# The hand-written order of tasks past the head is made anew (S5 scan and channel MLP, one Trainium2 core)

## The chip, the cores and the metric

The kernel runs on one core of one Trainium2 chip. The metric is device time in microseconds (us) of one execution. Five engines with a queue each carry the work: PE (TensorE, matmuls), ACT (ScalarE), DVE (VectorE), POOL (GpSimd) and SP (SyncE, which here only issues DMAs). An engine works through its own queue strictly in order. A wait on a semaphore at the head of a queue holds everything behind it.

## The reference, cut to what matters

```python
xn = layernorm(x)                                  # x: [1, 2048, 448], bf16
# s: a diagonal complex state space (P = 448)
Lam_bar = exp(dt * Lam);  B_bar = ((Lam_bar - 1) / Lam)[:, None] * B
h[t] = Lam_bar * h[t-1] + xn[t] @ B_bar.T
s = 2 * real(h @ C.T) + xn * Dskip
# g: a gated channel MLP, 448 -> 1792 -> 448
g = silu(gelu(layernorm(xn) @ w1 + b1) @ w2 + b2)
out = x + s * g
```

Matmul inputs are bf16, sums are f32.

## The kernel before

The 2048 rows are four groups of 512 (tasks of group g, g = 0 to 3). A group is two blocks b of 256 rows, and a block is 128 partitions times two neighbouring rows (par = 0, 1). The scan runs over pairs of rows, 256 columns a group. `x_all` holds x, in blocks x0 to x7.

For each group the kernel does this:

- Norms: statistics (`ln_stats`, DVE), scale factors (`ln_scale`, POOL or DVE: five instructions with a power on POOL, or a longer integer start and Newton steps on DVE), and the scaling (`ln_apply`, L451 on DVE, L452 on ACT) into `xn_sb` (first norm) and `xn2_sb` (norm of the norm). Both are transposed, mostly by DMA transposes that SP issues (`xt`, trace names xnT and xn2T; task keys xnT{g%2}_{b} and xmT{g%2}_{b}).
- `bu`: Bu in four tiles on PE (L643), copied by ACT out of PSUM bank 4 (L647). It needs BT, the transpose of B with a scaled copy LB beside it (`lb`, `combine` L586 to L596; `bt`, DMA transposes).
- `ssm`: with cos/sin tables W (`tables`, five sines on ACT at L580) the input is rotated (three passes over 1536 columns and two small ones on DVE, L660 to L664), scanned (seven `TENSOR_TENSOR_SCAN`, L668), copied to bf16 (ACT), and rotated back to h (L696 to L700). Between groups POOL turns the carry (cwk and cur, L682 to L694); the next group's scans need it.
- `mm1`: 14 tiles of 128 features of the MLP in seven steps j. Each step is two PE tasks: own halves of the contraction (tagged H{g}{j}) and the other halves. One ACT gelu of two tiles (L727) follows, into gT. Group 0 uses `mm1_half` (L731 to L745, one block at a time, without b1 in the activation, since b1 is a row of the weights there).
- `mm2`: per 128 rows 14 matmuls of 448 columns (L751) into PSUM bank 5 or 6 in turn, then on DVE the add of b2 (L754, reads the broadcast `b2bc`, and frees the bank), ACT's tanh (L755), and DVE's g (L756).
- `skip`: for par = 1 the term of Dskip: xd = xn * dbc, xr = xd * g, xr = xr + x, each on POOL (L767) or DVE (L768). `dbc` is the broadcast of Dskip, halved by ACT (task 44, L362).
- `ym`: the readout. For par = 0, h times CZ and xn times M0 (PE, L783 and L786); for par = 1, h times CQ (L789). Then t = psum * g (DVE, L792) and an add of x or xr (L795), and the store. CQ and CZ are combined from the transposes of C (`ct_dma`, Ct0 to Ct3, landing in `Cr`; `cq`, `combine`: a copy with a factor on ACT L593 or DVE L594, then a DVE multiply-add L596). M0 is one more product on PE (`m0`, L629), copied by ACT (L636).

How the order is set: every step is recorded as a task with the keys it reads and writes. Plain tasks are numbered in the order of their creation and a few carry names. `Plan.emit` takes the tasks in the list ORDER, appends each to its engine's queue, and puts ahead of it the waits on the semaphores of the tasks that it depends on. So ORDER fixes each engine's queue and nothing more. Tasks made with `either` have two forms on two engines; those listed in SECOND take the second one.

```python
plain = [t for t in self.tasks if t.tag is None]
for k in SECOND:
    plain[k].choose(1)
order = [plain[k] if isinstance(k, int) else self.named[k] for k in ORDER]
```

Names and numbers used below: B0 to B3 are the loads of b1 (SP); BF converts b1 to f32 on POOL (L359) and waits for them; 42 is the b2 broadcast load, issued from POOL's queue (L360); 43 the Dskip broadcast load, also from POOL, which waits for b2bc (L361); W is the load of the lower rows of w1 for the split tiles (SP). 70 to 87 are small table steps on POOL. 273 277 281 285 are the four mm2 tiles of group 0, 274 278 282 286 their b2 adds, 275 279 and so on the tanh. 234 236 238 240 are the four Bu tiles of group 0, 235 237 and so on ACT's copies of them. 369 is the other half of step H10 and 370 its gelu. 151 and 152 are the transposes xnT0_0 and xnT0_1, 320 and 323 those of group 1's second norm (xmT1_0, xmT1_1), 185 to 191 the transposes BT0 to BT6, 192 to 195 those of C, 182 to 184 the loads of C, 196 and 197 the loads of x4, x5 and x6, x7. 295 is the first readout of group 0, 405 that of group 1. 233 is the last part of CZ. 402, 290, 293, 399, 400, 403, 512 are steps of `skip`. 537 is the scale of group 3's norm. 427 is the scale of group 2's norm, which needs the statistics of x4 and x5.

Of the kernel before, what the change touches and what calls it, by code (L numbers as in the profile page):

```python
# [9 lines left out]
BF = dt.bfloat16  # L10
# [148 lines left out]


ORDER = [int(k) if k.isdigit() else k for k in """
0 9 18 22 10 1 19 23 16 20 15 89 2 11 21 3 26 27 12 8 17 14 13 24 5 25 7 6 90 28 4 46 29 91 97 92 30 98 93 99 31 94 47 32 95 100 49 50 48
104 96 54 33 101 51 55 102 53 34 103 56 63 106 115 35 52 57 107 36 117 108 109 37 64 110 65 66 38 119 105 39 116 40 58 118 121 41 59 67 111
120 B0 112 123 B1 122 149 147 B2 143 113 144 124 B3 125 114 45 148 127 156 61 126 155 62 154 60 150 73 153 129 157 128 131 130 161 158 168
133 160 132 170 135 171 134 159 186 137 136 169 BF 42 174 139 138 152 175 70 68 141 69 140 312 71 162 72 310 182 273 83 77 311 183 74 75 142
309 184 76 84 314 78 W 315 313 316 79 185 81 80 85 43 277 172 163 317 274 82 151 164 165 192 281 321 318 166 278 167 319 44 173 320 289 285
322 176 87 279 323 324 280 292 275 290 196 327 234 197 286 187 276 282 H10 235 193 177 145 H12 287 188 369 178 180 419 H11 328 370 179 189
373 420 422 423 371 190 H13 372 424 325 181 426 195 236 421 529 425 427 194 H14 237 374 375 191 288 238 431 428 429 432 H15 376 430 531 377
532 239 200 433 535 H16 378 379 243 329 381 530 283 240 242 382 326 533 H21 534 536 244 537 241 H20 201 198 481 204 380 199 479 205 330 202
245 293 208 541 387 246 203 331 253 538 542 206 207 146 262 209 332 482 263 539 399 540 210 383 251 86 88 264 543 333 211 480 388 291 252  # L170
212 389 248 222 249 284 247 334 213 250 214 384 335 256 257 223 254 258 259 265 220 336 260 266 402 294 215 268 H23 261 H24 226 390 221 485
216 395 224 217 225 267 269 228 255 385 229 391 396 232 270 227 486 386 339 218 337 392 271 230 434 233 338 H22 219 437 H26 340 483 491 231
487 343 492 348 295 345 393 484 H30 488 296 341 298 342 438 346 397 344 577 394 H31 349 435 351 H25 297 347 579 299 350 358 352 489 353 359
302 490 364 300 493 363 301 436 400 303 360 361 272 354 509 305 494 355 365 495 356 497 439 366 306 367 307 398 405 403 498 512 362 304 499
357 308 440 406 544 408 441 545 442 409 401 500 412 443 410 578 547 496 510 407 411 404 444 546 413 548 607 415 445 580 449 446 549 511 505
448 447 450 458 550 455 506 501 457 454 507 551 453 456 451 460 462 368 552 463 502 452 H32 553 459 H33 508 468 581 474 473 469 554 470 464
582 416 471 475 465 466 461 467 417 583 H35 584 476 477 513 H34 414 503 H36 478 555 610 559 585 472 587 586 558 589 588 556 560 515 565 590
566 564 595 514 516 568 567 517 563 518 570 591 519 520 557 596 521 418 561 522 562 573 504 592 593 597 603 569 571 523 572 594 525 574 598
599 524 604 526 575 576 527 605 616 528 600 608 601 606 613 609 617 618 611 628 612 620 614 615 602 619 629 624 630 621 631 622 625 623 626
627  # L180
""".split()]
SECOND = [int(k) for k in """
143 144 148 150 168 172 174 204 206 220 224 226 291 292 293 317 324 327 328 401 402 403 427 428 429 432 434 438 511 513 514 538 539 545 608 611 612 630
""".split()]


# [721 lines left out]
```

## Time and profile before

| what | value |
|---|---|
| time, median of 3 runs (lowest to highest) | 161.6 us (161.37 to 162.08) |
| the profiled execution's own time | 161.73 us |
| its span on the profile page | 160.0 us |
| granted clock of PE | 1.00 throughout |
| busy PE / DVE / ACT / POOL | 149.6 / 135.9 / 97.3 / 46.1 us |
| PE idle at 0 to 20, 20 to 50, 50 to 110, 110 to 150 us | 1.77, 4.68, 0.08, 0.67 us |
| PE's last matmul ends | 156.84 us |
| big loads and transposes landing: x2 and x3, C, x4, last BT | 19.7, 26.5, 37.1, 48.2 us |

Instruction times in the profile are the busy time of a group of instructions; a bracket after a row holds the idle time of the engine just before it and what ended that. The span runs from the first to the last recorded instruction; the time of a run is some 1.7 us longer.

### The profile page before, as it was taken

Reading aid. Unit: us, or ns where it says so; the run is one execution under the profiler, and the core shown is the slowest. Engines: PE = TensorE matmul, PEld = TensorE weight load, DVE = VectorE, ACT = ScalarE, POOL = GpSimd, SP = SyncE. Lnnn points to the kernel's source line nnn. Section 1 sums busy time; section 2 is a strip of 40 time slices with the busy share of each in tenths; the row PEclk is TensorE's granted clock in tenths of the full one; section 3 lists DMA queues with packets and bytes.
Section 4 is the critical chain, followed back from the end, with each engine's and each line's share of the span. In section 5 each row is a group of like instructions: output and inputs, shape, how many; then the busy total and the mean of one; then the engine's idle time right before and its main releaser. Section 6 shows DMA issues by size and latency. Waiting matters only on the chain.

```text
span 160.0 us, 3008 instructions
## 1 busy us (share of the span) xinstructions
PE 149.6 (94%) x1072; PEld 90.6 (57%) x1072; DVE 135.9 (85%) x287; ACT 97.3 (61%) x175; POOL 46.1 (29%) x120
## 2 busy tenths in 40 slices
PE   6999994979897999999999999998999999999992
PEld 6899952546554566655444445665566645555551
DVE  5899694679996898999998877959998889899984
ACT  3879896397559999646969651145435775424200
POOL 5572083230000905094000066309002660000111
DMA  4999999999999204300000023600700000030103
GB/s 122 291 291 370 229 227 182 144 204 265 209 135 184 39 0 66 69 0 0 2 4 0 0 79 64 64 27 15 157 0 6 0 0 4 0 117 0 57 0 117
DMA packets 31833, 14.97 MB, mean 94 GB/s; under 512 B 25285, under 2 KB 31305, under 8 KB 31818
## 3 DMA queue, kind: packets, MB, share of 16 engines
q1 hardware_dynamic: 31568, 14.49, 42.2%
q0 software_dynamic: 96, 0.23, 0.6%
q8 instruction: 8, 0.13, 0.3%
q10 hardware_dynamic: 154, 0.06, 0.1%
q14 instruction: 7, 0.06, 0.1%
HBM read 7.12 MB, written 1.84 MB: 56 GB/s over the span
## 4 chain that ended last, share of the span: by engine, by line
PE 40%; DVE 22%; DMA 13%; SPq 8%; ACT 6%; issue 5%; POOL 3%; POOLq 0%; ACTq 0%; DVEq 0%
PE psum L751 13%; PE psum L717 10%; PE psum L783 9%; SPq L90 7%; PE psum L643 5%; DMA b1b<-in_B_b_dram 4%; DMA b2bc<-in_B_b_dram 4%; DVE g_sb L756 3%; DMA Cr<-gT 3%; DMA dbc<-in_A_Dskip_dram 2%; PE psum L786 2%; DVE tmp L795 2%; DVE CZ L596 2%; DVE o L754 2%; DVE xr L768 2%
## 5 line engine op out<-in xcount | busy, mean ns | idle before, releaser
L751 PE MATMUL psum<-w_sb,gT 128*128 128x448 bf16 x224 | 44.5, 352 | 2.1 <-DVE o L754 2.1
L717 PE MATMUL psum<-xn2T,w_sb 64*128 64x512 bf16 x294 | 34.0, 378 | 2.2 <-ACT gT L727 1.2
L751 PEld LDWEIGHTS psum<-w_sb,gT 128*128 128x128 bf16 x224 | 21.7, 98 | 22.2 <-ACT WT L580 2.5
L727 ACT ACTIVATE gT<-psum,b1f 128x512 bf16<-128x512 f32 x42 | 26.2, 688 | 6.5 <-PE psum L717 4.5
L717 PEld LDWEIGHTS psum<-xn2T,w_sb 64*128 64x128 bf16 x294 | 16.1, 109 | 17.8 <-issue 4.3
L643 PE MATMUL psum<-xnT,BT 128*128 128x256 bf16 x196 | 24.1, 273 | 0.5 <-DMA BT<-Bn 0.5
L643 PEld LDWEIGHTS psum<-xnT,BT 128*128 128x128 bf16 x196 | 18.6, 98 | 6.5 <-issue 2.1
L755 ACT ACTIVATE th<-o 128x448 f32<-128x448 f32 x16 | 9.1, 576 | 16.9 <-DVE o L754 16.9
L668 DVE TENSOR_TENSOR_SCAN s_f<-cw,cur,v_sb 128x256 f32<-128x256 f32 x21 | 14.6, 735 | 0.2
L754 DVE TENSOR_TENSOR o<-psum,b2bc 128x448 f32<-128x448 f32 x16 | 9.9, 619 | 4.6 <-PE psum L751 2.4
L792 DVE TENSOR_TENSOR t<-psum,g_sb 128x448 bf16<-128x448 f32 (+2 forms) x17 | 9.9, 589 | 3.7 <-PE psum L789 2.7
L756 DVE SCALAR_TENSOR_TENSOR g_sb<-th,o 128x448 bf16<-128x448 f32 x16 | 11.0, 686 | 2.5 <-ACT th L755 2.5
L737 PE MATMUL psum<-xn2T,w_sb 128*128 128x256 bf16 x112 | 12.7, 273 | 0.4 <-DVE xn2T L408 0.3
L647 ACT ACTIVATE u_sb<-psum 128x512 bf16<-128x512 f32 x12 | 7.1, 593 | 9.6 <-PE psum L643 9.6
L737 PEld LDWEIGHTS psum<-xn2T,w_sb 128*128 128x128 bf16 x112 | 11.8, 111 | 0.9 <-issue 0.7
L783 PE MATMUL psum<-CZ,h_sb 128*128 128x448 bf16 x56 | 11.9, 353 | 0.0
L783 PE MATMUL psum<-CQ,h_sb 128*128 128x448 bf16 (+2 forms) x54 | 10.6, 332 | 0.7 <-DVE t L792 0.7
L767 POOL TENSOR_TENSOR xr<-x_all,xr 128x448 f32<-128x448 bf16 x3 | 3.9, 1312 | 20.6 <-DVE xr L768 20.6
L451 DVE TENSOR_SCALAR xn_sb<-x_all,lnw 128x448 bf16<-128x448 bf16 (+1 forms) x28 | 9.7, 384 | 0.1
L743 ACT ACTIVATE gT<-psum 128x512 bf16<-128x512 f32 x14 | 8.3, 594 | 2.1 <-PE psum L737 1.7
L682 POOL TENSOR_TENSOR cwk<-s_f,ang 128x3 f32<-128x3 f32 x3 | 0.7, 226 | 30.6 <-DVE s_f L668 30.6
L452 ACT ACTIVATE xn_sb<-x_all,lnw 128x448 bf16<-128x448 bf16 (+1 forms) x14 | 9.3, 685 | 0.0
(158 smaller groups left out, 225.3 us busy)
## 6 DMA issues: line engine op xcount, KB each, us to landing
out_dram<-tmp SPq DMA_DIRECT2D x7, 224.0 KB, 2.0
w_sb<-in_B_w_dram SPq DMA_DIRECT2D x3, 448.0 KB, 6.8
x_all<-in_A_x_dram SPq DMA_DIRECT2D x3, 448.0 KB, 5.2
w_sb<-in_B_w_dram SPq DMA_DIRECT2D x3, 384.0 KB, 4.7
w_sb<-in_B_w_dram SPq DMA_DIRECT2D x2, 224.0 KB, 6.8
gT<-in_A_C_re_dram SPq DMA_DIRECT2D x1, 392.0 KB, 4.6
Bn<-in_A_B_re_dram SPq DMA_DIRECT2D x1, 336.0 KB, 5.4
Bn<-in_A_B_im_dram SPq DMA_DIRECT2D x1, 336.0 KB, 5.4
```

What stands on the lines that cost most here:

```text
L90: return e.dma_start(out_ap, in_ap)
L451: on = [("dve", [lambda e, o=o, i=i: e.tensor_scalar(o, i, rs, nb, op0=ALU.mult, op1=ALU.add) for o, i in pairs], 0.4, 0.12), ("act", [lam ...
L643: fns = [lambda e, r=r, m=m, d=d: e.matmul(psum[:, 4, r * NK:(r + 1) * NK], BT[:, m, d, :], xnT[:, gx, d, :], start=(d == 0), stop=(d == 6 ...
L668: dve(lambda e, i=i, ri=ri, init=init: e.tensor_tensor_scan(s_f[:, i, ri, :], col(R2, i).to_broadcast([128, NK]), v_sb[:, i, ri, :], init, ...
L717: return lambda e: e.matmul(psum[:, b0 + k, :], w1_sb[halves[h], d, fcol(2 * j + k)], rhs[halves[h], d, :, :], start=first and d == 0, sto ...
L727: act([lambda e, k=k: e.activation(gT[:, gb, 2 * j + k, :], psum[:, b0 + k, :], ACT.Gelu_apprx_tanh, bias=b1f[:, 2 * j + k:2 * j + k + 1]) ...
L737: fns = [lambda e, k=k, d=d: e.matmul(psum[:, banks[k], :].rearrange("p (r c) -> p r c", r=2)[:, :, cs], w1_sb[:, d, fcol(2 * j + k)], rhs ...
L751: fns = [lambda e, fi=fi: e.matmul(psum[:, bk, 0:D], gT[:, gb, fi, q * 128:(q + 1) * 128], w2_sb[:, fi, :], start=(fi == 0), stop=(fi == N ...
L754: dve(lambda e: e.tensor_tensor(o2[:, fb, :], psum[:, bk, 0:D], b2bc[:], ALU.add), [f"ps{bk}", "b2bc"], [f"oo{fb}"], 0.62, prio - 76)
L756: dve(lambda e: e.scalar_tensor_tensor(out=g_sb[:, gs, :], in0=th[:, fb, :], scalar=1.0, in1=o2[:, fb, :], op0=ALU.add, op1=ALU.mult), [f" ...
L783: fns = [lambda e, k=k: e.matmul(psum[:, bk, c0:c1], h_sb[:, hb, k, k0:k0 + 128], cm[:, k, c0:c1], start=(k == 0), stop=False) for k in ra ...
L792: dve(lambda e: e.tensor_tensor(t3[:, fb, c0:c1], psum[:, bk, c0:c1], g_sb[:, gs, c0:c1], ALU.mult), [f"ps{bk}", f"g{gs}"], [f"t3{fb}_{c0} ...
```

## The change

Only ORDER past its head and SECOND change. No instruction's arithmetic, buffer or size changes; PE's queue holds the same tasks in another order. The first lines of ORDER with a change in what they issue, and SECOND:

```diff
-120 B0 112 123 B1 122 149 147 B2 143 113 144 124 B3 125 114 45 148 127 156 61 126 155 62 154 60 150 73 153 129 157 128 131 130 161 158 168
-133 160 132 170 135 171 134 159 186 137 136 169 BF 42 174 139 138 152 175 70 68 141 69 140 312 71 162 72 310 182 273 83 77 311 183 74 75 142
-309 184 76 84 314 78 W 315 313 316 79 185 81 80 85 43 277 172 163 317 274 82 151 164 165 192 281 321 318 166 278 167 319 44 173 320 289 285
...
+120 B0 112 123 B1 149 122 147 B2 143 113 144 B3 124 125 114 45 148 127 156 61 126 155 62 154 60 150 73 153 129 42 157 128 131 70 68 130 161
+69 158 168 71 133 160 72 132 83 170 77 74 135 171 75 134 76 84 159 186 137 78 136 169 79 81 174 80 162 139 82 85 183 184 87 BF 141 175 140
+182 172 138 277 43 309 185 142 88 86 313 312 310 151 316 173 163 314 273 311 152 164 278 315 176 317 188 165 285 192 178 274 321 W 145 322
...
-143 144 148 150 168 172 174 204 206 220 224 226 291 292 293 317 324 327 328 401 402 403 427 428 429 432 434 438 511 513 514 538 539 545 608 611 612 630
+143 144 148 150 162 168 174 176 178 180 206 208 230 289 294 317 318 321 324 325 328 401 404 427 428 429 431 435 437 438 509 537 538 539 542 544 545 607 608 610 630
```

The queues that follow from it, engine by engine:

```
POOL  before: 73 BF 42 70 68 69 71 72 83 77 74 75 76 84 78 79 81 80 85 43 82 289 87 290 537 ...
      after:  73 42 70 68 69 71 72 83 77 74 75 76 84 78 79 81 80 82 85 87 BF 43 88 86 292 256 293 257 290 402 258 259 260 263
              264 399 261 272 265 352 291 353 266 ...
SP    before: 45 186 152 182 183 184 W 185 151 192 320 323 196 197 187 193 188 189 190 195 194 191 430 433 329 326 540 543 ...
      after:  45 186 183 184 182 185 151 152 188 192 W 187 323 320 196 189 190 195 193 194 191 326 197 329 433 430 543 540 ...
PE    before: 273 277 281 285 234 H10 H12 369 H11 373 371 H13 236 H14 375 238 H15 377 H16 379 381 240 H21 H20 481 479 ...
      after:  277 273 285 234 281 236 H10 H11 369 H12 371 373 H13 238 H15 375 379 H14 240 H16 377 381 330 H21 H20 481 479 ...
```

On ACT the sines 163 to 167 stood together ahead of the dbc scaling (44); now five other steps lie among the first three and the fourth (two `combine` copies 176 and 178, two scalings of the norm 321 and 318, and 145, a diagonal for M0), 44 stands ahead of the fourth, and another copy (180) ahead of the fifth. In the middle of the kernel the first readout (295) stands ahead of H26 H22 491 483, where it stood behind them. Between the engines, nine tasks net leave DVE, ACT gets six more and POOL three more; the scale of group 3's norm (537) goes from POOL to DVE, the absolute value for the tables (162) from ACT to DVE, and the full-width passes of `skip` and of the final adds on POOL go from 13 to 17.

More of the change, by code (lines that the diff above doesn't have):

```diff
@@ L161 @@
 ORDER = [int(k) if k.isdigit() else k for k in """
-0 9 18 22 10 1 19 23 16 20 15 89 2 11 21 3 26 27 12 8 17 14 13 24 5 25 7 6 90 28 4 46 29 91 97 92 30 98 93 99 31 94 47 32 95 100 49 50 48
-104 96 54 33 101 51 55 102 53 34 103 56 63 106 115 35 52 57 107 36 117 108 109 37 64 110 65 66 38 119 105 39 116 40 58 118 121 41 59 67 111
-120 B0 112 123 B1 122 149 147 B2 143 113 144 124 B3 125 114 45 148 127 156 61 126 155 62 154 60 150 73 153 129 157 128 131 130 161 158 168
-133 160 132 170 135 171 134 159 186 137 136 169 BF 42 174 139 138 152 175 70 68 141 69 140 312 71 162 72 310 182 273 83 77 311 183 74 75 142
@@ L166 @@
-309 184 76 84 314 78 W 315 313 316 79 185 81 80 85 43 277 172 163 317 274 82 151 164 165 192 281 321 318 166 278 167 319 44 173 320 289 285
-322 176 87 279 323 324 280 292 275 290 196 327 234 197 286 187 276 282 H10 235 193 177 145 H12 287 188 369 178 180 419 H11 328 370 179 189
-373 420 422 423 371 190 H13 372 424 325 181 426 195 236 421 529 425 427 194 H14 237 374 375 191 288 238 431 428 429 432 H15 376 430 531 377
-532 239 200 433 535 H16 378 379 243 329 381 530 283 240 242 382 326 533 H21 534 536 244 537 241 H20 201 198 481 204 380 199 479 205 330 202
@@ L170 @@
[L170 to L177, printed above, removed]
@@ L178 @@
-566 564 595 514 516 568 567 517 563 518 570 591 519 520 557 596 521 418 561 522 562 573 504 592 593 597 603 569 571 523 572 594 525 574 598
-599 524 604 526 575 576 527 605 616 528 600 608 601 606 613 609 617 618 611 628 612 620 614 615 602 619 629 624 630 621 631 622 625 623 626
+0 9 18 22 10 1 19 23 16 20 15 89 2 11 21 3 26 27 12 8 17 14 13 24 5 25 7 90 6 28 4 91 29 97 92 30 46 98 93 99 31 94 47 32 95 100 49 50 48
+104 96 54 33 101 51 55 102 53 103 34 56 63 106 52 115 35 57 107 36 117 108 109 37 64 110 65 66 38 105 119 39 116 40 58 118 121 41 59 67 111
@@ new lines @@
+120 B0 112 123 B1 149 122 147 B2 143 113 144 B3 124 125 114 45 148 127 156 61 126 155 62 154 60 150 73 153 129 42 157 128 131 70 68 130 161
+69 158 168 71 133 160 72 132 83 170 77 74 135 171 75 134 76 84 159 186 137 78 136 169 79 81 174 80 162 139 82 85 183 184 87 BF 141 175 140
+182 172 138 277 43 309 185 142 88 86 313 312 310 151 316 173 163 314 273 311 152 164 278 315 176 317 188 165 285 192 178 274 321 W 145 322
+187 318 177 234 44 319 323 166 289 292 180 281 320 327 167 179 235 181 196 189 236 279 190 275 280 H10 237 286 195 193 328 276 H11 324 282
@@ new lines @@
+369 194 287 420 H12 421 370 424 422 371 419 325 373 288 191 H13 426 374 425 423 427 238 326 372 431 197 146 H15 239 329 428 432 375 243 379
+200 429 433 H14 376 242 240 430 201 198 244 H16 241 250 377 247 381 378 252 330 199 382 530 251 H21 331 249 380 H20 248 529 256 481 293 204
+531 479 202 245 257 290 402 283 203 332 254 532 258 206 246 535 387 482 259 260 284 437 205 536 207 333 208 210 383 533 253 209 211 220 268
+262 480 263 212 221 264 534 388 399 334 384 213 267 224 261 222 214 389 223 335 537 255 H24 H23 226 269 541 487 538 485 385 390 215 336 270
@@ new lines @@
+225 216 434 228 337 229 395 539 217 542 543 540 486 271 227 272 265 230 232 218 386 396 294 397 391 231 438 339 233 219 488 398 435 295 338
+392 340 H26 346 H22 296 345 491 344 H31 492 341 343 483 393 342 579 348 484 H30 394 347 298 350 352 291 H25 436 353 266 354 349 355 577 299
+351 489 364 302 358 297 490 363 359 356 360 365 578 357 497 303 300 301 361 400 305 401 498 366 493 439 306 509 304 544 307 367 403 405 494
+512 368 362 440 406 407 408 441 495 545 442 409 499 546 410 412 443 411 444 413 496 547 415 445 448 446 449 505 447 548 450 549 500 308 451
@@ new lines @@
+510 454 501 452 506 453 507 580 456 550 458 502 H34 459 508 461 H33 455 585 404 457 551 H32 468 416 462 460 463 469 583 607 470 581 584 464
+474 465 552 471 466 511 417 582 H36 473 472 513 553 586 H35 475 414 467 418 589 503 610 587 476 590 504 554 477 478 555 588 514 515 559 558
+556 560 595 557 516 567 565 518 596 566 597 591 561 564 519 562 598 520 603 517 568 521 563 592 570 569 522 608 593 573 609 571 604 599 523
+605 572 524 574 525 575 576 606 616 526 594 527 613 528 617 611 618 612 600 628 614 601 620 602 629 615 630 619 624 631 621 622 625 623 626
```

## The prediction

> **What bounds the kernel now.** I read the page first, then busy time by stage, then every idle stretch of PE with what ended it, then the POOL, ACT, DVE and SP timelines around those stretches.
>
> ```profile
> PE 149.6 (94%) x1072; PEld 90.6 (57%) x1072; DVE 135.9 (85%) x287; ACT 97.3 (61%) x175; POOL 46.1 (29%) x120
> 0.00:20.00 20.00, 18.23 (x178) 17.17 (x179) 15.90 (x48) 15.02 (x31) 8.88 (x47) 1.00 0.93 261
> 20.00:50.00 30.00, 25.32 (x185) 14.33 (x184) 23.04 (x72) 21.57 (x34) 6.97 (x22) 1.00 1.11 196
> 50.00:110.00 60.00, 59.92 (x412) 33.04 (x407) 52.84 (x95) 40.12 (x74) 20.52 (x35) 1.00 0.19 33
> 110.00:150.00 40.00, 39.33 (x264) 22.19 (x262) 36.69 (x60) 20.01 (x37) 7.86 (x15) 1.00 0.11 30
> 150.00:160.00 10.00, 6.84 (x44) 3.91 (x41) 7.44 (x15) 0.58 (x1) 1.84 (x2) 1.00 0.20 70
> ```
>
> The first line is the page's, the others the windows (stretch, length, then PE, PEld, DVE, ACT, POOL busy, granted clock, DMA share, GB/s). PE sets the time: it works 149.6 of 160.0 us at clock 1.00, and this edit changes no matmul. An order of tasks can only win PE's idle time: 4.68 us in 20 to 50, 0.08 in 50 to 110, 0.67 in 110 to 150, and the tail (PE ends at 156.84, the span at 160.0). The 1.77 before 20 us stands ahead of the edit. The third row warns: DVE is busy 52.8 of 60 beside a full PE, so a DVE queue in a worse order can become the bound there.
>
> Now the idle 4.68 us, in PE's timeline (start, length, operation, in brackets the idle time before it and what ended it):
>
> ```profile
> 27.07 5.46 PE L751 MATMUL psum<-w_sb,gT 128*128 128x448 bf16 x28 [2.12 <-DVE o L754]
> 36.03 4.73 PE L717 MATMUL psum<-xn2T,w_sb 64*128 64x512 bf16 x42 [0.54 <-DVE o L754]
> 41.24 1.70 PE L643 MATMUL psum<-xnT,BT 128*128 128x256 bf16 x14 [0.48 <-DMA BT<-Bn]
> 49.01 2.34 PE L717 MATMUL psum<-xn2T,w_sb 64*128 64x512 bf16 x20 [1.16 <-ACT gT L727]
> ```
>
> The largest, 2.12, is a PSUM bank that the add of b2 (L754) had not freed. POOL says why, and ACT has a gap of the same family:
>
> ```profile
> 19.54 0.20 POOL L359 CAST b1f<-b1b 128x14 f32<-128x14 bf16 x1 [6.30 <-DMA b1b<-in_B_b_dram]
> 20.08 0.82 POOL L90 DMA_DIRECT2D b2bc<-in_B_b_dram  x1 [0.35 <-issue]
> 26.57 0.59 POOL L90 DMA_DIRECT2D dbc<-in_A_Dskip_dram  x1 [1.71 <-DMA b2bc<-in_B_b_dram]
> 30.43 0.58 ACT L362 ACTIVATE dbc<-dbc 128x448 bf16<-128x448 bf16 x1 [3.74 <-DMA dbc<-in_A_Dskip_dram]
> 31.02 1.28 ACT L755 ACT_TABLE_LOAD   x1
> b2bc<-in_B_b_dram POOLq DMA_DIRECT2D x1, 112.0 KB, 6.2
> dbc<-in_A_Dskip_dram POOLq DMA_DIRECT2D x1, 112.0 KB, 3.8
> ```
>
> POOL stood 6.30 us at the conversion of b1 (BF) for its DMA, with the b2 broadcast (task 42) queued behind it. b2bc landed at 26.27, dbc (43, which waits for b2bc) at 30.41, and ACT idled 3.74 before scaling dbc (44), ahead of the tanh of the first gate.
>
> **The change, part by part.** *b2 ahead of BF.* POOL reaches 42 at about 13.3, where it now starts to wait. With its measured flight of 6.2 (bounds: 3.8, dbc's, and 7.2, the longest row of the issue list, b1b's) it lands at 19.5 (17 to 20.5). The first add of b2 is wanted when PE ends its first MLP tile, about 23 to 23.6. So the 2.12 goes, with 3 us to spare; each us past 24.2 would cost one. BF now comes behind a block of table steps, at about 20 (b1b landed at 19.32); its first reader is the first gelu past the head, at 37.9 now: free, with 17 us of cover. 43 follows at 20 to 21.3 and lands at 24 to 27.5; ACT gets to 44 at about 28.3. The 3.74 of ACT goes too, but not all as gain: ACT receives combine copies and scalings between its sines (0.66, 0.66, 1.09, 0.39, 1.09, 1.34, less 1.05 and 0.67 that leave it), so the sine table ends at 31.3, not 26.69, then the u copy of 234, the tanh table load (1.28) and the first tanh at 33.2 to 33.7, against 32.32.
>
> *PE, 22 to 50.* The order is now 277 273 285 234 281 236 H10 … (27x, 28x are mm2 tiles of 2.73 each, 23x Bu tiles of 1.70, H1x halves of mm1). 285 ends at about 27.5, 234 at 29.1, 281 at 31.8; 236 waits 0.2 for ACT's copy of 234's PSUM and ends at 33.6, and H10 starts there. Before, H10 started at 34.44 with 236 still ahead: 0.84 + 1.70 = 2.5 won by then. Later waits of 0.54, 0.48 and 1.16 are gone in the new order by hand (the transposes of B for 236 to 240 and of C now leave SP with several us in hand), and one comes: H13 waits for the first gelu of group 1, about 0.8. Left of the 4.68 is 1.0: **−3.7**. This needs xmT1 (second norm, transposed) by 33.6. Its two transposes now follow BT4, Ct0, W and BT1 on SP; by SP's issue times (1.23 to 1.7 each, one at 2.31 as below) I get 33 to 34.6, against 33.55 and 34.34 now, worst 36: cost 0 to 2.4, taken 0 as the issues are mostly of the short kind.
>
> ```profile
> 23.23 2.31 SPq L89 DMA_TRANSPOSE xnT<-xn_sb  x1
> ```
>
> *50 to 78.* Loads x4 to x7, their statistics, the CQ and CZ combines and the scan now share DVE in a new order; 537 (scale of group 3, 1.97) comes to it from POOL, nine tasks net leave it over the whole kernel (about −3.4 us of work). PE needs CZ6 (task 233) complete before its readout 295, which starts at 83.48 now and stands 3.05 us of PE work earlier in the new queue. 427, the scale of group 2's norm, ends at about 41.5 (x4 lands at 36.6, now 37.09, by SP's order between 35.5 and 37.5; then four statistics steps, a gate and the scale itself, 4.9). From there to 233 DVE has 14 combines of 0.60 (8.4), 7 scans of 0.60 (4.2), 11 norm steps of 0.5 (5.5), 1.97 for 537, 7 adds and gates of 0.53 (3.7), 7 large passes of 0.87 (6.1) and small ones (2.5): 32.4 us. Add 0.75 of waiting for an ACT copy and what POOL's full-width passes do to DVE:
>
> ```profile
> 57.94 0.58 DVE L451 TENSOR_SCALAR xn_sb<-x_all,lnw 128x448 bf16<-128x448 bf16 x2
> 60.11 1.32 DVE L451 TENSOR_SCALAR xn_sb<-x_all,lnw 128x448 bf16<-128x448 bf16 x2
> 60.20 1.20 POOL L767 TENSOR_TENSOR xd<-xn_sb,dbc 128x448 bf16<-128x448 bf16 x1
> 72.43 1.34 DVE L596 SCALAR_TENSOR_TENSOR CZ<-Cr,cw,tmp 128x448 bf16<-128x448 bf16 x1
> ```
>
> The same DVE form takes 0.58 alone and 1.32 beside the POOL pass at 60.20, and 0.68 became 1.34 beside a second one at 72.07; over the twelve such passes of this trace the mean loss is 0.33, as most meet DVE operations that lose nothing. Four passes fall here: 1.4. 41.5 + 32.4 + 0.75 + 1.4 gives 76.1; PE is at 295 at 83.48 − 3.05 − 3.7 = 76.7. Bounds of the loss 0 (as summed) to 2 (x4 landing 2 us later); **+0.5**, nearer zero since the sum has 0.6 in hand.
>
> [...]
>
> *78 to 110.* The last scan of group 1's second half waits for a POOL carry that now sits behind two other steps and a 1.2 pass: 1.6 us late on DVE; a DVE add waits for POOL's xr; PE's 405 needs the last h, about 0.25 ahead by the sum. 0 to 2, **+0.7**, the middle being nearer to that 0.25.
>
> *110 to 160.* PE's only idle stretch (0.67 at 111.0, waiting for a DVE product behind task 407) goes, as 407 stands earlier: **−0.7**. The final h of group 3 is ready at 144.7 by sums, PE wants it at 145.4: 0 to 0.5, **+0.2**. From the last readout's start to the end is 10.15 now and its DVE chain is the same: 0.
>
> **Sum.** −3.7 + 0.5 + 0.7 − 0.7 + 0.2 = −3.0. The profiled execution took 161.73 (span 160.0), 0.1 over the median 161.6, less than the runs' own spread: 158.7 us.
>
> **Rivals.** *POOL in DVE's way (slower).* Full-width POOL passes rise from 13 to 17 and eight lie between 50 and 110 us, where DVE has no slack in the new order. If each blocks DVE for its own length, 1.2 in place of 0.35, that adds 8 × 0.85 = 6.8, giving 165.5; half of it where every second one meets scans, 162.1. Slower than now by 0.8 from a mean of 0.82 a pass. For it: the two collisions above. Against: ten other passes cost little. [...]
>
> *SP and DMA too late (no change).* SP is one queue in order, DMA share is 1.11 in 20 to 50, and x4's load now waits in line behind the first C transpose and xmT1. If C's transpose waits for its source (C landed at 26.54) and each later one takes 2.31 rather than 1.3, xmT1 comes at 36 to 37 and x4 at 39: PE loses 2.4 there, and the middle 0.5 to 1.5: 161.1 to 162. From H10 at 37.5 on nothing is left. Against: the issues of 1.23 to 1.33 are the rule in SP's timeline.
>
> *The b2 broadcast does not do what it says.* If POOL's early issue waits or the flight, now among the weight loads (DMA share 0.93 in 0 to 20), grows to 12 us, b2bc lands at 25.2 and 0.9 comes back: 159.6; at 14 us, 161.6, no gain left. The flights of 4.3 to 7.2 of loads issued in those 20 us speak against it. [...]
>
> *No loss in the middle.* DVE's sums hold: 158.7 − 1.4 = 157.3, and 156.6 if the 0.8 at H13 and its fellows vanish as well.
>
> **How the numbers follow.** This kernel's measurement can tell 0.5% (0.8 us) from no change. Forecast 0.58 (its own range 157.0 to 160.4: 1.7 either way, which is the two middle terms and the end at nearly nothing, or at 3.1 in place of 1.4); no middle loss 0.08; b2 late 0.09 (0.06 faster, 0.03 same); SP late 0.12 (0.10 same, 0.02 slower); POOL in the way 0.13 (slower). Faster 0.72, same 0.13, slower 0.15. The range runs from the lossless case less 0.2, 156.4, to half the POOL case, 162.2, leaving out most of that rival and little else.
>
> **What would show it.** Right: 42 issued near 13.3 and landed by 20; no idle stretch of PE over 0.3 between 20 and 32 us; ACT without a gap before L362; H10 at 33 to 34.5; idle of PE in 20 to 50 near 1.0 and in 50 to 110 near 1.2, with DVE named as releaser; no wait at 111. Wrong: H10 past 36 with "DMA xn2T" as releaser (SP rival); DVE operations at twice their length beside every POOL pass and PE idle over 3 us in 50 to 110 (POOL rival); b2bc landing past 24 us.

## The result and the profile after

Over 20 executions each, the ratio of the new order to the old is 0.9898, 95% interval 0.9862 to 0.9934: 1.0% faster (0.7 to 1.4%), 1.6 us of 162. The medians are 160.24 us (158.92 to 162.58) and 162.75 us; they lie further apart than the ratio because the ratio leaves disturbed executions out, and the old kernel had more of them. The profiled execution took 160.29 us with a span of 158.5, against 161.73 and 160.0. The forecast was faster by 3.0 us to 158.7. The sign was right; the size was about twice what came.

The stages after, in the windows view (stretch, length, PE, PEld, DVE, ACT, POOL busy, granted clock, DMA share, GB/s):

```profile
0.00:20.00 20.00, 18.16 (x178) 17.08 (x179) 16.80 (x49) 14.43 (x31) 14.68 (x57) 1.00 0.93 262
20.00:50.00 30.00, 27.25 (x202) 15.34 (x200) 23.12 (x67) 26.90 (x45) 4.05 (x14) 1.00 1.10 196
50.00:110.00 60.00, 59.01 (x403) 33.47 (x402) 48.57 (x99) 39.27 (x72) 15.25 (x30) 1.00 0.20 36
110.00:150.00 40.00, 39.62 (x261) 22.13 (x260) 38.34 (x61) 19.64 (x37) 10.31 (x16) 1.00 0.08 24
```

PE's idle time goes from 4.68 to 2.75 us in 20 to 50, from 0.08 to 0.99 in 50 to 110, and from 0.67 to 0.38 in 110 to 150. The tail (3.12 us from PE's end to the span's, 3.16 before) and the start (1.84, 1.77) stay. That is 1.28 us won of the 1.5 by which the span is shorter; the remaining 0.2 is in the recorded matmul time (149.41 for 149.63).

PE's timeline names the waits of after:

```profile
28.91 1.69 PE L643 MATMUL psum<-xnT,BT 128*128 128x256 bf16 x14 [1.28 <-DMA xnT<-xn_sb]
34.35 1.69 PE L643 MATMUL psum<-xnT,BT 128*128 128x256 bf16 x14 [1.10 <-DMA BT<-Bn]
36.41 5.71 PE L717 MATMUL psum<-xn2T,w_sb 64*128 64x512 bf16 x50 [0.37 <-DMA xn2T<-xn_sb]
50.53 1.69 PE L643 MATMUL psum<-xnT,BT 128*128 128x256 bf16 x14 [0.47 <-issue]
52.74 3.21 PE L717 MATMUL psum<-xn2T,w_sb 64*128 64x512 bf16 x28 [0.53 <-DMA xn2T<-xn_sb]
130.21 1.50 PE L783 MATMUL psum<-CZ,h_sb 128*128 128x448 bf16 x7 [0.39 <-DVE h_sb L700]
```

The four waits of before that the prediction shows (two on adds of b2, one on a transpose of B, one on a gelu) are gone. In their place stand waits on DMA transposes: xnT0_1 landed at 28.82, BT1 at 34.21, xmT1_0 at 36.27, xmT0_0 at 52.61, each just before the matmul that it releases. The profile marks the 0.47 at 50.53 as issue (a wait with no releaser found); a transpose of xn landed at 50.44.

POOL and ACT of after show that the b2 part did what it was to do:

```profile
13.60 1.14 POOL L90 DMA_DIRECT2D b2bc<-in_B_b_dram  x1
21.90 0.20 POOL L359 CAST b1f<-b1b 128x14 f32<-128x14 bf16 x1
22.08 0.62 POOL L90 DMA_DIRECT2D dbc<-in_A_Dskip_dram  x1
28.35 0.56 ACT L362 ACTIVATE dbc<-dbc 128x448 bf16<-128x448 bf16 x1
33.01 1.04 ACT L755 ACTIVATE th<-o 128x448 f32<-128x448 f32 x2
```

b2bc lands 6.5 us after its issue, at 20.1, POOL has no wait at the conversion, and ACT reaches L362 without one.

### The profile page after: what moved, and what is told of

The parts are those of the page before. It is cut to its first block, busy times and chain, and to the rows that moved or that the text cites. A ratio compares the mean times of both kernels' runs of the same rounds, so it can differ in the third digit from the quotient of the medians.

```text
span 158.5 us, 3022 instructions
## 1 busy us (share of the span) xinstructions
PE 149.4 (94%) x1072; PEld 91.1 (57%) x1072; DVE 132.6 (84%) x285; ACT 100.8 (64%) x183; POOL 47.3 (30%) x119
## 3 DMA queue, kind: packets, MB, share of 16 engines
HBM read 7.12 MB, written 1.84 MB: 56 GB/s over the span
## 4 chain that ended last, share of the span: by engine, by line
PE 52%; DVE 16%; DMA 9%; ACT 9%; SPq 8%; issue 4%; ACTq 0%; DVEq 0%
PE psum L751 17%; PE psum L783 12%; PE psum L717 9%; SPq L90 8%; PE psum L643 7%; DMA x_all<-in_A_x_dram 4%; PE psum L786 4%; PE psum L632 3%; DMA BT<-Bn 3%; DVE s_f L668 3%; ACT gT L727 2%; DMA xn2T<-xn_sb 2%; ACT xn_sb L452 2%; DVE lnst L382 1%; DVE h_sb L698 1%
## 5 line engine op out<-in xcount | busy, mean ns | idle before, releaser
L717 PE MATMUL psum<-xn2T,w_sb 64*128 64x512 bf16 x294 | 33.7, 377 | 0.9 <-DMA xn2T<-xn_sb 0.9
L717 PEld LDWEIGHTS psum<-xn2T,w_sb 64*128 64x128 bf16 x294 | 16.8, 109 | 15.9 <-issue 2.9
L668 DVE TENSOR_TENSOR_SCAN s_f<-cw,cur,v_sb 128x256 f32<-128x256 f32 x21 | 15.9, 776 | 1.8 <-POOL cur L694 1.7
L452 ACT ACTIVATE xn_sb<-x_all,lnw 128x448 bf16<-128x448 bf16 (+1 forms) x18 | 11.8, 685 | 4.5 <-DVE xd L768 4.1
L767 POOL TENSOR_TENSOR xr<-xd,g_sb 128x448 f32<-128x448 bf16 x7 | 7.3, 1049 | 22.3 <-DVE g_sb L756 12.6
L756 DVE SCALAR_TENSOR_TENSOR g_sb<-th,o 128x448 bf16<-128x448 f32 x16 | 9.8, 613 | 1.9 <-ACT th L755 1.9
L382 DVE BATCH_NORM_STATS2 lnst<-x_all 128x6 f32<-128x448 bf16 x14 | 8.1, 610 | 2.6 <-DMA x_all<-in_A_x_dram 2.5
L767 POOL TENSOR_TENSOR xr<-x_all,xr 128x448 f32<-128x448 bf16 x5 | 6.4, 1286 | 12.1 <-DVE xr L768 12.0
```

Of the source, the lines that this page charges most:

```text
L452: ("act", [lambda e, o=o, i=i: e.activation(o, i, ACT.Identity, bias=nb, scale=rs) for o, i in pairs], 0.75, 0.2)]
L668: dve(lambda e, i=i, ri=ri, init=init: e.tensor_tensor_scan(s_f[:, i, ri, :], col(R2, i).to_broadcast([128, NK]), v_sb[:, i, ri, :], init, ...
L717: return lambda e: e.matmul(psum[:, b0 + k, :], w1_sb[halves[h], d, fcol(2 * j + k)], rhs[halves[h], d, :, :], start=first and d == 0, sto ...
L756: dve(lambda e: e.scalar_tensor_tensor(out=g_sb[:, gs, :], in0=th[:, fb, :], scalar=1.0, in1=o2[:, fb, :], op0=ALU.add, op1=ALU.mult), [f" ...
L767: kb.either(("pool", lambda e, o=o, i0=i0, i1=i1, op=op: e.tensor_tensor(o, i0, i1, op), 1.37, 0.15), ("dve", lambda e, o=o, i0=i0, i1=i1, ...
```

## The experiments

The question was where the other 1.5 us went. Theory A at first: SP's in-order issue sets when transposes land, and the b2 broadcast hid that. Theory B: only b2 counts. Theory C: the load on the DMA engines sets the landings. Theories D and E came later. Each kernel was timed in five rounds beside the old one; ratios are to the old kernel of the same batch. Landings and waits are of one profiled execution each. Two executions of the changed kernel itself had xnT0_1 at 28.82 and 29.98, and BT1 at 34.21 and 34.87, so one such difference of up to 1.2 us does not tell two kernels apart. The queues name tasks: 185 to 191 are BT0, BT3, BT1, BT4, BT2, BT5, BT6 in that order.

**The changed kernel again**, as a yardstick.

> The changed kernel once more, as the yardstick of this batch. Both theories: ratio to the kernel before near 0.990 (0.986 to 0.993), span near 158.5, PE waits of about 1.3 ahead of the first Bu tile, 1.1 ahead of the second and 0.4 ahead of H10, all ended by DMA transposes.

Ratio 0.9931 (0.9898 to 0.9965), which overlaps the interval of the first batch. Its profile is of an execution of 161.41 us, in which the first wait was 2.01 us instead of 1.28; the section on the hardware comes back to it.

**b2 alone, in the old order.**

```diff
 POOL: 73
-BF 42
+42 BF
 70 68 ...
```

> The kernel before with one edit: the b2 broadcast is issued ahead of the b1 conversion on POOL; everything else as before. Theory A (the issue order of SP's transposes bounds the head; b2 only hid it): the 2.12 us wait at 27 us goes, but H10 still waits for the second-norm transposes of group 1 (landed at 34.34 before), so nearly all of it comes back as a wait there: span 159.5 to 160.0, ratio 0.997 to 1.000. Theory B (b2 is the lever, transposes have slack): the 2.1 to 2.7 us stay won: span 157.4 to 157.9, ratio 0.984 to 0.987.

Ratio 0.9933 (0.9901 to 0.9966), span 158.1. One swap of two tasks gives as much as the whole new order of the same batch. The result lies between the theories: the ratio is outside both ranges, the span nearer to B's. The wait at 27 us only shrinks. PE's rows of this kernel:

```profile
25.56 5.46 PE L751 MATMUL psum<-w_sb,gT 128*128 128x448 bf16 x28 [0.85 <-DVE o L754]
32.76 1.06 PE L717 MATMUL psum<-xn2T,w_sb 64*128 64x512 bf16 x8 [0.22 <-issue]
47.12 2.34 PE L717 MATMUL psum<-xn2T,w_sb 64*128 64x512 bf16 x20 [1.18 <-ACT gT L727]
```

H10 moves from 34.44 to 32.76, because DVE was held too. In the old kernel (first row) the add waits for b2bc with the scalings of xm0 and xm1 queued behind it; with b2 early (second row) it runs as soon as the scale before it is done. DVE's timeline of the old kernel, then of this one:

```profile
26.29 0.62 DVE L754 TENSOR_TENSOR o<-psum,b2bc 128x448 f32<-128x448 f32 x1 [1.99 <-DMA b2bc<-in_B_b_dram]
```

```profile
24.79 0.62 DVE L754 TENSOR_TENSOR o<-psum,b2bc 128x448 f32<-128x448 f32 x1
```

So xmT1's transposes, which theory A held fixed, came 1.7 us earlier as well (32.67 for 34.34), and H10 starts 0.09 us after the last of them. Theory A had missed that they too waited for b2, by way of DVE's queue.

**b2 undone, in the new order.**

```diff
 POOL: 73
+BF
 42 70 68 69 71 72 83 77 74 75 76 84 78 79 81 80 82 85 87
-BF
 43 88 ...
```

> The changed kernel with one edit: the b1 conversion stands ahead of the b2 broadcast on POOL again, the new order otherwise. Theory A: PE waits about 1.8 us ahead of its third mm2 tile, but the waits for transposes that follow (1.28, 1.10, 0.37) shrink by as much, H10 starts at 36.4 to 37: span 158.5 to 159.2, ratio to the kernel before 0.990 to 0.995. Theory B: 2.1 to 2.7 us lost, ratio 1.003 to 1.007.

Ratio 0.9983 (0.9954 to 1.0013), span 159.0. PE waits 1.64 at 27.12 us; the next two waits shrink to 1.01 and 0.42, the one ahead of H10 is gone, and 0.38 for a gelu comes at 42.41. The new order without b2 is worth nothing that can be told from zero. In the new order b2 and the transposes are two bounds side by side: PE's idle time from 20 to 110 us is 3.53 without b2 and 3.74 with it. The 0.5% between the two ratios is at the limit of what these runs can tell, as their intervals overlap.

**The transposes of xn ahead of BT3.** SP stood from 14.24 to 17.04 for BT3's source; the two transposes of xn had theirs at 14.0.

```diff
 SP: 45
+151 152
 186 183 184 182 185
-151 152
 188 ...
```

> The changed kernel with one edit on SP: the two transposes of xn of group 0 (sources ready at 14.0 us) stand ahead of the transpose BT3, for whose source SP waits from 14.24 to 17.04. Theory A (SP's in-order issue, back to back from 17 to 50 us, sets the landings): all later transposes are issued 2.6 to 2.8 us earlier, the waits 1.28, 1.10, 0.37, 0.47 and 0.53 of PE go for the most part: span 155.8 to 156.8, ratio 0.973 to 0.981; if DVE is then late for the first readout, up to 1 us of it comes back there. Theory C (the DMA engines' load sets the landings, the order of issue does not): landings stay within 0.5 us, span 158.0 to 158.6, ratio 0.986 to 0.991.

Ratio 0.9965 (0.9924 to 1.0005), span 158.5: no gain. SP's row:

```profile
13.81 5.74 SPq L89 DMA_TRANSPOSE xnT<-xn_sb  x2
```

The free slot was none: among the weight loads the two issues took 5.74 us, not 2.6. BT0, now behind them, landed 3.0 us later (28.41), BT1 only 0.7 earlier (33.47) and xmT1_0 0.2 earlier (36.11). PE waited 0.72 for BT0 in place of xnT.

**Two transposes of C moved ahead** of BT1 and xmT1.

```diff
 SP: ... 192 W
+195 193
 187 323 320 196 189 190
-195 193
 194 ...
```

> The changed kernel with two of the transposes of C (195, 193) moved on SP ahead of BT1 and of the two second-norm transposes of group 1; the sum of the work is the same. Theories A and C: BT1 and xmT1 land 2.6 us later, the second Bu tile and H10 start 2.4 to 2.7 us later; the later waits of 0.47 and 0.53 do not change or go: span 160.0 to 161.2, ratio 1.000 to 1.007. Theory B: under 0.7 us, ratio 0.990 to 0.997.

Ratio 1.0103 (1.0037 to 1.0169), span 161.0. BT1 landed at 36.55 and xmT1_0 at 39.30, 2.3 and 3.0 us later: 1.2 to 1.5 us for each transpose put ahead. The span also holds a drop of PE's clock behind the long wait (last section).

```profile
36.68 2.62 PE L643 MATMUL psum<-xnT,BT 128*128 128x256 bf16 x14 [3.68 <-DMA BT<-Bn]
```

**The loads of C off SP**, onto ACT's queue.

```diff
-ld("sp", Cn[0:112, ...
+ld("act", Cn[0:112, ...
 SP:  ... 186
-183 184 182
 185 151 ...
 ACT: ... 174
+183 184 182
 140 ...
```

> The changed kernel with the three loads of C issued from ACT's queue in place of SP's (1.65 us off SP between BT3 and BT0, some 1.5 us onto ACT; the bytes for the DMA engines are the same). Theory A (what stands ahead on SP in order sets when a transpose lands): BT0, the transposes of xn, BT1 and the second norm are issued and land 1 to 1.7 us earlier, PE's waits 1.28, 1.10 and 0.37 sum to 0.8 to 1.6: span 156.9 to 157.9, ratio 0.981 to 0.989. Theory C (the DMA engines' work): landings within 0.5 us of the changed kernel's, ratio 0.990 to 0.994.

Ratio 0.9882 (0.9827 to 0.9937), span 157.8. BT0 was issued 1.69 us earlier and landed 0.3 later (25.69 for 25.40); xnT0_1 landed 0.2 and BT1 0.3 earlier. Theory A in its plain form falls: SP ran ahead, the landings did not follow. The time is at the slow end of theory A's range, but no earlier landing of xn's transposes carries it.

**Most of C's bytes taken away**, SP's issues kept.

```diff
-ld("sp", Cn[0:112, :, o:o + n], dram_ap(cm, a, [[D, 112], [112 * D, 4], [1, n]]) ...
+ld("sp", Cn[0:8, :, o:o + n], dram_ap(cm, a, [[D, 8], [112 * D, 4], [1, n]]) ...
-kb.dma("sp", Cr[...], Cn[0:112, d, 0:896], reads=CK + GA ...
+kb.dma("sp", Cr[...], w2_sb[0:112, 2 * d:2 * d + 2, :] ..., reads=CK + GA + (the w2 loads) ...
```

> The changed kernel with the loads of C cut to 8 of 112 partitions (the same three DMAs stay in SP's queue); the transposes of C read rows of w2 instead, so the readout is not that of C. It takes about 4 us of work off the DMA engines between 18 and 25 us and nothing off SP. Theory C (the DMA engines' work before 52 us sets when transposes land): the transposes of xn, BT1 and the second norm land 2 to 4 us earlier, the waits 1.28, 1.10, 0.37 of PE shrink to under 0.8 in all: span 156.0 to 157.3, ratio 0.975 to 0.985. Theory A (SP's issues by themselves, about 1.3 us each, set the landings): landings and span as in the changed kernel, 158.2 to 158.8, ratio 0.990 to 0.994.

Ratio 0.9877 (0.9821 to 0.9932), span 157.8, between the ranges of the two theories. xnT0_1 landed at 29.63, later than before the cut (28.82); BT1 and xmT1_0 0.9 and 0.7 earlier. So these bytes alone did not hold the transposes of xn either.

What was left in flight at 23 to 28 us was the Skip broadcast, which the new order issues at 22.08. The clusters of long transpose packets that the next expectation names are no sign of it: they come at 25 us too where no broadcast is in flight (up to 0.93 us in dbc_memset, 0.61 in c_dbc_cut), and near 19, 31 and 45 us (up to 1.07, 2.26 and 1.44 us in the changed kernel).

**The Skip broadcast left out** (theory D), and **left out together with C's bytes**.

```diff
-ld("pool", dbc[:], dram_ap(A_Dskip, 0, [[0, 128], [1, D]]), ["dbc"], 114688, -20, reads=["b2bc"])
+pool(lambda e: e.memset(dbc[:], 1.0), ["b2bc"], ["dbc"], 0.5, -20)
```

> The changed kernel with the broadcast load of Dskip (dbc) left out and a constant written by POOL in its place, so the skip term is not Dskip's. In the profiles the few transpose packets that take 0.3 to 2 us (18 ns is their usual time) come in clusters, some while dbc is in flight (24 to 27 us). Theory D (that broadcast holds the transposes up): the transposes of xn land 0.8 to 2 us earlier (26.8 to 28.0), PE's first wait of 1.28 goes to 0 to 0.5: span 157.0 to 158.0, ratio 0.982 to 0.989. Theory E (the transposes' own work and other traffic hold them, dbc counts for nothing): landings within 0.4 us, ratio 0.989 to 0.994.

Ratio 0.9842 (0.9788 to 0.9895), span 157.4. xnT0_1 landed at 27.48, 1.3 us earlier, and the wait of 1.28 ahead of the first Bu tile is gone, as theory D said; 1.62 remains ahead of the second, where BT1 is the input that landed last (33.24; the profile names ACT).

> The same with the loads of C cut to 8 of 112 partitions too (as in c_tiny2): from 20.5 to 28 us only transposes are left on the DMA queues. Theory C (bytes of the loads) with D: the transposes of xn land by 25 to 26.5, waits of PE under 0.5 in 20 to 36: span 155.8 to 157.0, ratio 0.974 to 0.983. Theory E (each transpose costs about 1.3 us of a pipeline of its own, and what stands ahead of it in that pipeline sets its landing): no better than c_tiny2, transposes of xn at 27.5 to 29.5: span 157.5 to 158.3, ratio 0.985 to 0.992.

Ratio 0.9771 (0.9725 to 0.9818), span 156.3. The transposes of xn land at 26.06 and 26.83; waits of 0.89 and 0.33 remain, on BT1 and xmT1. The time is theory C's, the waits are not: C's bytes now buy 1.1 us of span more, and a rest stays. One load is still beside BT1 there: W, 224 KB, stands directly ahead of it on SP (in the changed kernel W is in flight from 28.37 to 33.44, BT1 from 28.96 to 34.21). No run moved W.

**The Skip broadcast issued earlier, nothing left out.** It stands right behind the b2 broadcast, in place of behind BF.

```diff
-..., ["dbc"], 114688, -20, reads=["b2bc"])
+..., ["dbc"], 114688, -20, reads=["sgn3"])
 POOL: 73 42
+43
 70 68 ... 85 87 BF
-43
 88 ...
```

> The changed kernel with the Skip broadcast issued on POOL right behind the b2 broadcast (near 15 us, no longer waiting for it), so that its 112 KB move among the weight loads and not beside the transposes of xn; nothing is left out. Theory D (that broadcast in flight holds the transposes): the transposes of xn land at 26.5 to 27.7, PE's wait ahead of the first Bu tile falls from 1.28 to under 0.4: span 157.3 to 158.1, ratio 0.982 to 0.989. If the broadcast takes the same time from the loads of w2 or x2, x3 that it gives back to the transposes: PE waits over 0.5 before 22 us, or statistics of group 1 start over 0.5 later, ratio 0.989 to 0.994.

Ratio 0.9840 (0.9781 to 0.9899), span 157.4. POOL's issue of it, and three of PE's waits:

```profile
14.05 0.61 POOL L90 DMA_DIRECT2D dbc<-in_A_Dskip_dram  x1
28.03 1.69 PE L643 MATMUL psum<-xnT,BT 128*128 128x256 bf16 x14 [0.43 <-issue]
33.49 1.69 PE L643 MATMUL psum<-xnT,BT 128*128 128x256 bf16 x14 [1.13 <-DMA BT<-Bn]
35.52 5.75 PE L717 MATMUL psum<-xn2T,w_sb 64*128 64x512 bf16 x50 [0.34 <-DMA xn2T<-xn_sb]
```

xnT0_1 lands at 27.94. The price is paid where nobody waits for long: x2 and x3 land 0.5 us later (20.78). PE's five gaps up to 53 us sum to 2.65 in place of 3.75, and the span is 1.1 shorter, with the same bytes. By these profiles the broadcast's place beside the transposes cost 1.1 us, and leaving it out won no more. The ratio's interval overlaps that of the changed kernel, from another batch, so the times alone would not carry this. The landings do: with the broadcast issued at 21.3 to 22.1, xnT0_1 landed between 28.57 and 29.98 (the changed kernel twice, two_c_ahead, c_on_act, c_tiny2); without it there, between 26.83 and 27.94 (dbc_memset, c_dbc_cut, dbc_early). The 1.1 us itself is a difference of single profiles.

**The transposes of xn on PE.** Seven small matmuls each into PSUM bank 7, and a DVE copy (L473), in place of two DMA transposes.

```diff
-xt(0, b, 0, "dma", -59)
+kb.tag = f"X{b}"; xt(0, b, 0, "dve", -59, bank=7)
 PE:  141 +X0 277 +X1 273 ...        SP: -151 -152
 DVE: 172 +151 309 ... 173 +152 314 ...
```

> The changed kernel with the two transposes of xn of group 0 done by PE (7 small matmuls each, PSUM bank 7) and copied by DVE (0.6 us each), not by DMA: it takes two transposes off SP and off the DMA engines and puts 0.9 us on PE. Theories A and C both: landings from BT4 on 2.5 to 3.5 us earlier, waits of PE in 20 to 53 us fall from 3.75 to 0.5 to 1.0, less 0.9 for the matmuls: span 156.4 to 157.2, ratio 0.976 to 0.984. A third theory, B (only the b2 broadcast counts, any other gain of the head is given back in the middle because DVE is then the bound for the first readouts): PE waits over 1 us in 50 to 110 for DVE, span 158 to 159, ratio 0.990 to 0.996.

Ratio 0.9851 (0.9798 to 0.9904). Its profile had slow matmuls before 14 us (40 in 6.28 us, 4.53 in the changed kernel), so it was run again:

> The kernel of xnt_on_pe again, for a profile without the slow matmuls that the first one had before 14 us (40 matmuls in 6.28 us where the changed kernel took 4.53) and for a narrower interval. Theory C: PE's first tile of mm2 starts near 19.9, waits of PE in 20 to 53 us 0.5 to 1.2 in all, span 156.3 to 157.2, ratio 0.978 to 0.986. Theory B (DVE gives the gain back in the middle): waits over 1 us in 50 to 110.

Ratio 0.9842 (0.9794 to 0.9890), span 156.5, the shortest of the kernels that leave nothing out. BT1 landed at 30.13 and xmT1_0 at 33.29, 4.1 and 3.0 us earlier. The head of PE has no wait on a DMA left; of the 0.75 us idle in 20 to 50, 0.27 is for an add of b2 and 0.36 for a gelu (windows):

```profile
20.00:50.00 30.00, 29.25 (x224) 16.39 (x221) 25.25 (x70) 27.97 (x48) 3.29 (x10) 1.00 1.01 196
50.00:110.00 60.00, 59.96 (x406) 33.26 (x404) 49.23 (x99) 38.54 (x71) 15.68 (x30) 1.00 0.13 29
```

PE's timeline shows seven of the small matmuls, the first Bu tile and the first tiles that read xmT1, none with a wait ahead of it:

```profile
22.54 0.56 PE L467 MATMUL psum<-ident,xn_sb 128*128 128x128 bf16 x7
28.23 1.69 PE L643 MATMUL psum<-xnT,BT 128*128 128x256 bf16 x14
34.33 2.57 PE L717 MATMUL psum<-xn2T,w_sb 64*128 64x512 bf16 x22
```

This order and the earlier Skip broadcast were not tried together. Theory B falls: PE is ahead of the changed kernel by 2.1 us at the first readout, and still nothing in 50 to 110 waits. It had the DVE chain come along, as x4's load follows these transposes on SP (35.75 for 38.45).

Two transposes more ahead (two_c_ahead) and two fewer (xnt_on_pe2) change SP's queue and the DMA engines' work together, so they do not say which of the two sets the 1.2 us or more that a transpose costs.

**The same with b2 undone.**

```diff
 POOL: 73
+BF
 42 70 68 ... 85 87
-BF
 43 88 ...
```

> The kernel of xnt_on_pe with the b1 conversion ahead of the b2 broadcast again. If the b2 add and the transposes are two bounds side by side, each hiding the other, then with the transposes out of the way the late b2 costs its full price: PE waits 1.5 to 2.2 us ahead of its third mm2 tile and nothing behind absorbs it: span 158.0 to 158.8, ratio 0.993 to 1.000. If b2 is worth no more here than in the changed kernel (0.5%), the ratio is 0.987 to 0.991.

Ratio 0.9955 (0.9902 to 1.0007). PE waits 2.10 us ahead of its third mm2 tile and nothing behind it absorbs that: b2, worth 0.5% in the changed kernel, is worth 1.1% here (two batches; the intervals of this kernel and of xnt_on_pe2 do not overlap). The span of 159.8 is above what was expected: a drop of PE's clock behind the wait made the tile 1.7 us longer (last section), so not all of it is the wait.

**The old order with b2 early and the transposes of xn on PE.**

```diff
-xt(0, b, 0, "dma", -59)
+kb.tag = f"X{b}"; xt(0, b, 0, "dve", -59, bank=7)
 POOL: 73
-BF 42
+42 BF
 PE:  141 +X0 273 +X1 ...        SP: -151 -152
 DVE: 312 +151 ... 316 +152 ...
```

> The old order with two edits only: the b2 broadcast ahead of the b1 conversion, and the two transposes of xn of group 0 on PE (copied by DVE). Theory C: here PE reaches the Bu tiles late, behind all four mm2 tiles, so it does not wait for them; what can go is the wait of 1.18 before H16 (a gelu that waits for the last transposes of C), and 0.9 us of matmuls come: span 157.6 to 158.3, ratio 0.989 to 0.994, no better than b2_alone. If it is better than 0.986, the old order had more waits on the DMA engines than its profile names.

Ratio 0.9958 (0.9918 to 0.9998), span 158.4: no better than b2 alone, as expected, and a little worse than the range given. The old order reaches the Bu tiles late, so it has no use for early transposes. The new order is what makes them worth something.

## Why the prediction was right and wrong, step by step

*b2 ahead of BF* was right where it counts: issue at 13.3 (13.60), landing at 19.5 (20.1), ACT at dbc at 28.3 (28.35), the first tanh at 33.2 to 33.7 (33.01), no cost from BF. BF and 43 came later than forecast (21.90 and 22.08, for about 20 and 20 to 21.3), and dbc landed at 27.92 (24 to 27.5); nothing waited for that. The 2.12, 0.54, 0.48 and 1.16 of before are gone, as said.

*"Left of the 4.68 is 1.0: −3.7"* is the step that failed. What is left is 2.75, and 0.99 more at 50.5 and 52.7: −0.94 in place of −3.7. The term that it had wrong is the wait for DMA transposes, put at nothing. No landing was set against "285 ends at about 27.5, 234 at 29.1"; xmT1 alone had bounds, with the cost "taken 0". 285 ended at 27.64, and then PE waited 1.28 for xnT0_1, 1.10 for BT1 and 0.37 for xmT1_0, which came at 36.27, past its worst case of 36.

The old trace held the warning. xnT0_0 landed there at 29.45 and BT1 at 39.74; the old order read them at 32.36 and 41.24, the new one wants them near 27.5 and 32. And H10 stood on xmT1 already. The prediction's four rows sum to 4.30 of the 4.68; the row that it leaves out starts 0.10 us after xmT1_1 landed, at 34.34:

```profile
34.44 1.06 PE L717 MATMUL psum<-xn2T,w_sb 64*128 64x512 bf16 x8 [0.38 <-issue]
```

The clause "the transposes of B for 236 to 240 and of C now leave SP with several us in hand" counted issues; in the changed kernel the landings came 2.8 to 6.4 us behind them. The likely wait at H13 (0.8) did not come.

The cause, as far as it is shown: the head moves at the pace of a stream of transposes. One more in front costs those behind 1.2 to 1.5 us (two_c_ahead), two fewer give 3.0 to 4.1 (xnt_on_pe2). What else is in flight beside them counts on top. The Skip broadcast, which the change itself moved from 26.57 to 22.08, cost about 1.1 us (dbc_early), and C's bytes 1.1 once it was gone (c_dbc_cut), each by a pair of profiles. The prediction followed 43 only to ACT; the bytes of the moved DMA were not priced. Open is what sets the pace of the stream, and the 0.89 and 0.33 that remain without these two loads.

*The middle, +0.5 and +0.7*, was wrong the other way: it cost nothing. CZ6's multiply-add ended at 78.82, and the first readout began at 79.28:

```profile
78.14 0.68 DVE L596 SCALAR_TENSOR_TENSOR CZ<-Cr,cw,tmp 128x448 bf16<-128x448 bf16 x1
79.28 1.49 PE L783 MATMUL psum<-CZ,h_sb 128*128 128x448 bf16 x7
88.98 0.75 DVE L668 TENSOR_TENSOR_SCAN s_f<-cw,cur,v_sb 128x256 f32<-128x256 f32 x1 [1.68 <-POOL cur L694]
```

The slack was 0.46 us; the sum by hand had 0.6. Both came 2.6 us or more later than forecast. With PE 2.1 us earlier (xnt_on_pe2) it was 0.40, as the DVE chain came 2.05 earlier too: both hang on the same stream, since x4 lands behind the transposes. That this kept the slack was not foreseen. The last row is the scan that waits for POOL's carry: 1.68 measured, 1.6 forecast. It was there, but off the path.

*The rest.* The wait at 111 went (−0.67). The final h, forecast at 0.2, cost nothing at the end; another h did at 130 (0.39), which the prediction did not have, so that the two sizes are near each other is luck. The tail is as before.

*The sum by what was measured*: −0.94 − 0.67 + 0.38 = −1.2, of 1.5 in the span.

*The rivals.* "SP and DMA too late" came nearest: it had xmT1 at 36 to 37 and x4 at 39 (36.27 and 38.45) and a loss of 2.4 for PE. Its price of 161.1 to 162 was too high because it added middle losses that did not come. Part of its agreement is luck: it had the first transpose of C wait for its source, and C landed at 24.50, before that transpose was issued at 27.05. It deserved more than 0.12, as the old trace showed its landings. POOL in DVE's way did not show: no wait of PE in 50 to 110 names DVE, and DVE's busy time there fell from 52.84 to 48.57. The b2 rival did not either: the flight was 6.5 us, with DVE busy for 6.39 of them, against 6.2 before with 3.89; only the issue was longer, 1.14 us for 0.82 (0.78 in dbc_early).

## What to carry to other kernels

When a wait goes away, look up in the old trace when each later input of that engine landed, not when it was issued: those landings can be the next bound, hidden so far by the old wait or the old order. A DMA that a reorder moves carries its bytes along, so price whom it now flies beside (here 112 KB, about 1.1 us by one pair of profiles). And try the single cheapest part of a reorder alone: here one swap in one queue gave as much as all the rest with it.

## What the runs showed of the hardware

**The granted clock dropped after some waits of about 2 us.** After waits of 2.01 us (the changed kernel's second profile) and 2.10 us (xnt_pe_b2_undone), PE ran at half its clock: the granted clock was 0.73, 0.50 and 0.91 in 30 to 32, 32 to 34 and 34 to 36 us of the first, and 0.63 and 0.52 in 28 to 30 and 30 to 32 us of the second. By an estimate from these windows that is some 3.4 us at half clock each time (from 30.9 to 34.4, and from 28.5 to 32.0). Windows of the second kernel, where the third number from the end is the granted clock (the stretch begins while the tile runs):

```profile
28.00:30.00 2.00, 2.00 (x9) 0.87 (x7) 1.73 (x10) 0.29 (x1) 0.22 (x2) 0.63 1.21 248
30.00:32.00 2.00, 2.00 (x7) 0.79 (x6) 1.38 (x4) 2.00 (x6) 0.00 (x0) 0.52 0.37 63
```

Its mm2 tile in PE's timeline:

```profile
27.70 4.49 PE L751 MATMUL psum<-w_sb,gT 128*128 128x448 bf16 x14 [2.10 <-DVE lnmv L386]
```

The tile took 4.49 us where 2.81 is usual, 1.7 us on top of the wait. It does not follow every wait of that length: behind the old profile's 2.12 and the 1.83 of c_tiny2 the tiles kept their usual length (5.46 us for two, 1.69). The 3.68 of two_c_ahead had one (0.81, 0.50 and 0.83 in 36 to 38, 38 to 40 and 40 to 42 us, by the same estimate from 37.2 to 40.7). What decides after which wait the clock drops was not shown. The three profiled executions with such a drop have a mean granted clock of 0.987 to 0.989. Of the changed kernel's 20 executions the five with 0.989 are the five longest (161.26 to 162.58 us; the others 158.92 to 160.79). That a drop made them longer is likely, but not shown by traces of theirs.

**The issue of a transpose has no fixed length.** On SP it took 1.22 to 2.21 us in the changed kernel; two issued among the weight loads took 5.74 together (xnt_first). What sets the length was not shown.

**A group of POOL's small table steps took 0.92 us in one kernel and 2.69 in the other.** The group of four at L522 took 2.69 us at 17.46 in the changed kernel, where DVE was at passes of 448 and 1024 columns (0.44 to 1.22 us each, the longest L572 at 17.92), and 0.92 at 22.53 in the old one, where DVE was at the small steps of `ln_scale` (0.17 to 0.22 us each). In c_tiny2, xnt_on_pe2 and dbc_early it took 1.48, 1.72 and 2.69. That DVE's passes made the difference was not shown. PE did not wait for it here.
